# A retention layer and two gated layers on one core: two batches' attention and u ahead of their v, in a listed order

## The chip, the cores and the metric

The kernel runs on one core of a Trainium2 chip. The metric is the device time of one execution in microseconds, as the median of several runs. The core's engines (TensorE, VectorE, ScalarE, GpSimd, SyncE; PE, DVE, ACT, POOL, SP in the rows) run their own instruction lists in order and wait for each other by semaphores.

## The reference

Eight batches of 576 tokens, eight heads of 64; all in float32 (the weights come as float64).

```python
scores = scale * np.matmul(q, k.transpose(0, 1, 3, 2))
Dmat = np.where(rel >= 0, gamma[:, None, None] ** rel[None, :, :], 0.0)
x = transpose(np.matmul(scores * Dmat, v))        # [8, 576, 512]
h = gelu_tanh(x @ w_in)                           # 512 -> 1024
u, v = h[..., :512], h[..., 512:]
v_n = (v - mean(v)) / np.sqrt(var(v) + 1e-06) * g_ln
v_s = np.einsum('ts,bsd->btd', w_sg, v_n) + b_sg[None, :, None]
x = x + (u * v_s) @ w_out
gate = sigmoid(causal_conv(x, conv_w))            # 5 taps
out = gate * (x @ w_val) @ w_out2
```

## The kernel before, in words

Every product is made in float32r with the operands split into a high and a low part: high times high, high times low, low times high, so 12 matmuls for 512 input columns. The float64 weights are decoded to such pairs on the chip (`decode`, L122): two passes on ScalarE (absolute value, and the copy of the high part) and eight on VectorE.

**First part** (to about 440 us), for each batch:
- *Attention* in three groups of 192 tokens (group i is batch i // 3), in chunks of 64 tokens. Per group: `load_kq` and `load_v` (two buffers each), `k_decay` (12 or 8 small ScalarE operations), `q_decay`, `scores` (the products q k, tile sc, and the chunks' state sums, tile st), `masked` (sc by the decay mask, tile pt, one buffer), `states`, `state_decay` (all VectorE), `outputs` (tile xo, one PSUM buffer), `out_copy` (ScalarE, to the one staging buffer xg), `out_high` (ScalarE, the high part of x, and the store x1d, issued by SyncE), `out_low` (VectorE). `burst(i)` (L381) is outputs of group i, then scores of group i + 1.
- *u*: eight tiles (`u_tile`, 12 matmuls of 288 columns, and `u_gelu`). Tile n takes a quarter of a half of w_in's columns and one half of the tokens; quarters 0 and 1 of w_in (256 columns each) hold u, quarters 2 and 3 hold v.
- *v*: four tiles of 128 tokens, and one for the last 64 tokens of two batches (`v_tile`, 12 matmuls of 512 columns), each with gelu, statistics (VectorE and GpSimd), normalisation and split; vt has two buffers.
- *Mix*: eight tiles (`mix`, 14 matmuls of 288 columns, over w_sg split in ws and wr) and `gate` (VectorE), stored to g1d.

The two PSUM buffers of `ps_g` serve all tiles of u, v and mix.

**The order.** The head is written out by hand (L507 to L642): decode of quarter 0, attention of groups 0 to 2 between the decodes of quarters 1 to 3, the eight u tiles of batch 0, and v of batch 0 between the bursts of groups 3 and 4. From there a planner (`plan`, L641) gives every step a place in TensorE's time and sorts: the list `slow` (v and u of batch 1, then for each batch b mix b, v and u of b + 2), with the bursts at the places of `PLACES`, counted in steps from mix b. The planner also puts the split of w_sg into v of batch 1 and the decode of the second weights (`decode_second`, two of twelve pieces of w_out, w_val, w_out2 per batch) into u.

**Second part**: nine blocks of 512 tokens with the three remaining products, the convolution and the gate. TensorE never waits there until the end.

Of the kernel before, what the change touches and what calls it, by code (L numbers as in the profile page):

```python
# [44 lines left out]
def fused_kernel(  # L45
# [48 lines left out]
    with ExitStack() as p1:  # L94
# [23 lines left out]
        ws = one.tile([128, 2, 4, S], F32R, name="ws")  # L118
# [3 lines left out]
        def decode(dst_hi, dst_lo, src, a, s, t, like=lambda x: x):  # L122

            low, high = src[:, :, 0], src[:, :, 1]
            af, sf, tf = a.bitcast(F32), s.bitcast(F32), t.bitcast(F32)

            yield act.activation(af, high.bitcast(F32), AF.Abs)
            dve.tensor_scalar(af, af, _as_f32(896 << 20), _as_f32((1150 << 20) + 0xFF000), op0=ALU.max, op1=ALU.min)

            dve.tensor_scalar(a, a, 3, 0x40000000, op0=ALU.logical_shift_left, op1=ALU.bitwise_xor)  # L130
            dve.tensor_scalar(s, high, 31, 31, op0=ALU.logical_shift_right, op1=ALU.logical_shift_left)
            yield dve.scalar_tensor_tensor(a, a, 0x7FFFF000, s, op0=ALU.bitwise_and, op1=ALU.bitwise_or)

            dve.tensor_scalar(t, high, 0x1FF, None, op0=ALU.bitwise_and)
            yield dve.scalar_tensor_tensor(tf, t, 2.0**32, low, op0=ALU.mult, op1=ALU.add)
            dve.tensor_scalar(s, a, 23, 23, op0=ALU.logical_shift_right, op1=ALU.logical_shift_left)
            yield dve.scalar_tensor_tensor(dst_lo, like(tf), 2.0**-52, like(sf), op0=ALU.mult, op1=ALU.mult)
            yield act.copy(dst_hi, like(af))

        def run(steps, n=9):  # L140
            for _ in range(n):
                if next(steps, None) is None:
                    break
# [5 lines left out]
        def fetch_w_in(g):  # L149
            sync.dma_start(out=raw_in[:, g % 2].rearrange("p n t -> p (n t)"), in_=w_in[g])  # L150

        def decode_w_in(g):
            cols = slice(g * 256, (g + 1) * 256)
            return decode(
                wi[:, 0, :, cols],
                wi[:, 1, :, cols],
                raw_in[:, g % 2],
                *(tmp_in[:, i] for i in range(3)),
                like=lambda x: x.rearrange("p (k c) -> p k c", k=KT),
            )  # L160
# [4 lines left out]
        raws = {}  # L165
# [6 lines left out]
        def load_conv():  # L172
            n = KT * TAPS
            both = dec.tile([128, 2, n], F32, tag="cw", name="cw")
            run(decode(both[:, 0], both[:, 1], raws.pop("conv")[:, :n], *small_tmp(n)))
            dve.tensor_tensor(cw_sb.rearrange("p k t -> p (k t)"), both[:, 0], both[:, 1], op=ALU.add)
# [4 lines left out]
        def decode_second(j):  # L181
            raw = raws.pop(j)
            t = raw.rearrange("p n t -> p (n t)").rearrange("p (t n) -> p t n", t=2).bitcast(F32)
            yield from decode(t[:, 0].bitcast(F32R), t[:, 1].bitcast(F32R), raw, *small_tmp(DM))
            yield sync.dma_start(out=w2d[:, j // KT, :, j % KT], in_=t)
# [28 lines left out]
        def load_kq(i):  # L214
            if i < NGR:
                t = grp[i] = {}
# [35 lines left out]
        def scores(i):  # L252
# [4 lines left out]
            a, k, v = t["a"], t["k"], t["v"]  # L257
            st = t["st"] = ps_a.tile([128, 2, 512], F32, tag="st", name="st")
            sc = t["sc"] = ps_a.tile([128, 2, 512], F32, tag="sc", name="sc")
            for j in range(GC):  # L260
                at = slice(j * CK, (j + 1) * CK)
                for f in range(2):
                    for o, c in four:
# [5 lines left out]
                        )  # L269
            for j in range(chunks(i)):  # L270
# [86 lines left out]
        def out_high(i):  # L357
            b, g = divmod(i, NG)
            if g == 0:
                x = bt[b] = dict(  # L360
                    xh=mid.tile([128, KT, S], F32R, tag="xh", name="xh"),
                    xl=mid.tile([128, KT, S], F32R, tag="xl", name="xl"),
                )
                x["xr"] = (
                    bt[b - 1]["xr"]
                    if b % 2
                    else [mid.tile([128, KT, 128], F32R, tag=f"xr{j}", name="xr") for j in range(2)]
                )
# [3 lines left out]
            sync.dma_start(out=x1d[:, :, b * S + g * GT : b * S + (g + 1) * GT], in_=xc)  # L372
# [97 lines left out]
        mx = {}  # L470

        def mix(b, i):
# [3 lines left out]
            vh, vr = t["vh"], t["vr"]  # L476
# [3 lines left out]
            for s in range(4):  # L480
                a, l = vh[:, 0, s, cols], vh[:, 1, s, cols]
                wh, wl = ws[:, 0, s, t0 : t0 + n], ws[:, 1, s, t0 : t0 + n]
                for lhs, rhs in ((a, wh), (a, wl), (l, wh)):
                    pe.matmul(ps[:, :n], lhs, rhs, start=first, stop=False)  # L484
                    first = False
            for j in range(2):
                pe.matmul(ps[:, :n], vr[:, cols], wr[:, j, t0 : t0 + n], start=False, stop=j == 1)  # L487
# [17 lines left out]


        fetch_w_in(0)  # L507
        sync.dma_start(out=kf_sb, in_=kfac)
        load_kq(0)
        sync.dma_start(out=dm_sb, in_=dmask)  # L510
        load_v(0)
        sync.dma_start(out=qf_sb, in_=qfac)
# [472 lines left out]
```

## Time and profile before

| | us |
|---|---|
| median of 3 runs | 759.81 (759.77 to 760.47) |
| profiled execution | 759.48 |
| its span, first to last instruction | 757.6 |
| TensorE busy in the span | 723.0 |
| VectorE busy | 513.7 |
| ScalarE busy | 332.5 |

Mean granted clock of TensorE: 0.981 of 2.4 GHz. TensorE is busy in 95% of the span, and the rest is not spread evenly: in the page's 40 slices, those after 125 us show it busy throughout and at full clock, and those before show gaps and, from 15 to 45 us and around 80 and 91 us, the lower clock. Busy time counts a matmul at the lower clock at its full length.

### The profile page before, as it was taken

To read this page: it belongs to the slowest core of one execution; us is meant where nothing else is said; L and a number is where in the kernel's file an instruction comes from. 1 tells how busy PE (TensorE), PEld (TensorE's weight loads), DVE (VectorE), ACT (ScalarE), POOL (GpSimd) and SP (SyncE) were. 2 spreads that over 40 slices of the span, in tenths; PEclk is the share of its full clock that TensorE was granted. 3 is DMA by queue.
4 is the path that set the end of the run, shared out by engine and by line. 5 is a ranking of instruction groups with operands and counts; after the bars stand their busy time and mean duration, and the time that the engine had idled before them with its cause. 6 is when DMAs were issued, how large, how long until landed. Compare 5 with 4: busy or idle time off the path is not lost.

```text
span 757.6 us, 18035 instructions
## 1 busy us (share of the span) xinstructions
PE 723.0 (95%) x7804; PEld 631.8 (83%) x7804; DVE 513.7 (68%) x890; ACT 332.5 (44%) x638; POOL 51.4 (7%) x123
## 2 busy tenths in 40 slices
PE   6499789999999999999999999999999999999998
PEld 6487679989899799898998998888888888888886
DVE  5964658676576686775764369997876858667512
ACT  4545854454452734653336206444543425243321
POOL 0001120020210200301103000000000000000000
PEclk9689899999999999999999999999999999999999
DMA  9963745848518658476143683331404322010111
GB/s 357 380 197 128 241 152 181 298 163 285 178 62 278 213 181 301 134 250 240 56 138 134 249 291 141 136 143 56 166 32 136 93 75 104 7 56 1 55 56 55
DMA packets 54718, 121.21 MB, mean 160 GB/s; under 512 B 3952, under 2 KB 25584, under 8 KB 53744
## 3 DMA queue, kind: packets, MB, share of 16 engines
q1 hardware_dynamic: 49024, 104.87, 40.6%
q10 hardware_dynamic: 5184, 8.92, 3.1%
q0 software_dynamic: 432, 6.29, 2.2%
q8 instruction: 61, 1.00, 0.5%
q14 instruction: 17, 0.14, 0.1%
HBM read 85.46 MB, written 34.60 MB: 158 GB/s over the span
## 4 chain that ended last, share of the span: by engine, by line
PE 81%; DVE 5%; ACT 5%; DMA 4%; issue 2%; POOL 1%; SPq 0%; ACTq 0%; DVEq 0%; POOLq 0%
PE ps_back L89 13%; PE ps_out L89 13%; PE ps_val L89 13%; PE ps_m L484 13%; PE ps_u L89 12%; PE ps_v L395 8%; PE ps_m L487 2%; PE xo L335 2%; PE xo L327 2%; DMA qk_sb<-in_qk 2%; PE sc L265 2%; PE st L274 2%; DMA x1d<-xg 1%; ACT vt L429 1%; ACT vt L412 1%
## 5 line engine op out<-in xcount | busy, mean ns | idle before, releaser
L89 PE MATMUL ps_u<-xh,wi 128*128 128x288 f32 x512 | 108.9, 302 | 6.9 <-ACT vt L412 4.7
L484 PE MATMUL ps_m<-ws,vh 128*128 128x288 f32 x768 | 113.5, 296 | 0.1
L834 DVE SCALAR_TENSOR_TENSOR gate<-x,cw_sb,gate 128x516 f32<-128x516 f32 (+1 forms) x144 | 103.3, 748 | 6.2 <-ACT gate L832 5.1
L484 PEld LDWEIGHTS ps_m<-ws,vh 128*128 128x128 f32 x768 | 105.1, 188 | 1.2 <-DVE gt L494 0.6
L89 PE MATMUL ps_out<-gv,wv 128*128 128x512 f32 x432 | 102.3, 395 | 0.0
L89 PE MATMUL ps_val<-xs,wv 128*128 128x512 f32 x432 | 102.3, 395 | 0.0
L89 PE MATMUL ps_back<-gs,wo 128*128 128x512 f32 x432 | 102.0, 395 | 0.0
L89 PEld LDWEIGHTS ps_val<-xs,wv 128*128 128x128 f32 x432 | 81.3, 188 | 19.3
L89 PEld LDWEIGHTS ps_out<-gv,wv 128*128 128x128 f32 x432 | 81.3, 188 | 19.2
L89 PEld LDWEIGHTS ps_back<-gs,wo 128*128 128x128 f32 x432 | 81.1, 188 | 19.5
L89 PEld LDWEIGHTS ps_u<-xh,wi 128*128 128x128 f32 x512 | 85.1, 192 | 9.9 <-ACT vt L412 6.0
L395 PE MATMUL ps_v<-wi,xh 128*128 128x512 f32 x256 | 83.1, 407 | 3.0 <-ACT xh L69 1.5
L89 PE MATMUL ps_u<-xl,wi 128*128 128x288 f32 x256 | 76.7, 300 | 2.2 <-DVE xl L72 2.2
L395 PEld LDWEIGHTS ps_v<-wi,xh 128*128 128x128 f32 x256 | 48.5, 194 | 14.3 <-ACT xh L69 2.1
L494 DVE SCALAR_TENSOR_TENSOR gt<-ps_m,g_sb,b_sb 128x288 f32<-128x288 f32 x64 | 33.0, 516 | 40.3 <-PE ps_m L487 40.3
L849 DVE TENSOR_TENSOR gvf<-ps_val,gate 128x512 f32<-128x512 f32 (+7 forms) x64 | 26.6, 452 | 47.5 <-PE ps_val L89 47.5
L832 ACT ACTIVATE gate<-x,cw_sb 128x516 f32<-128x516 f32 (+1 forms) x36 | 25.9, 725 | 64.0 <-DVE x L815 64.0
L69 ACT CAST gv<-gvf 128x512 fp32r<-128x512 f32 x36 | 22.3, 620 | 68.6 <-DVE gvf L849 67.6
L420 DVE BATCH_NORM_STATS2 stat<-vt 128x6 f32<-128x512 f32 x36 | 25.0, 693 | 40.4 <-ACT vt L412 40.2
L395 PE MATMUL ps_v<-wi,xl 128*128 128x512 f32 x128 | 51.5, 402 | 0.3 <-DVE xl L72 0.3
L412 ACT ACTIVATE vt<-ps_v 128x512 f32<-128x512 f32 x36 | 21.5, 597 | 68.4 <-PE ps_v L395 61.3
L89 PEld LDWEIGHTS ps_u<-xl,wi 128*128 128x128 f32 x256 | 49.1, 192 | 2.7 <-DVE xl L72 2.5
(88 smaller groups left out, 1012.4 us busy)
## 6 DMA issues: line engine op xcount, KB each, us to landing
qk_sb<-in_qk SPq DMA_DIRECT2D x24, 960.0 KB, 7.9
vv_sb<-in_vv SPq DMA_DIRECT2D x24, 576.0 KB, 4.3
kk_sb<-in_kk SPq DMA_DIRECT2D x24, 384.0 KB, 5.1
x1d<-xg SPq DMA_DIRECT2D x24, 384.0 KB, 7.4
g1d<-u SPq DMA_DIRECT2D x16, 576.0 KB, 6.7
graw<-g1d SPq DMA_DIRECT2D x9, 1024.0 KB, 5.6
xraw<-x1d SPq DMA_DIRECT2D x9, 1024.0 KB, 5.1
out<-o ACTq DMA_DIRECT2D x32, 256.0 KB, 2.0
```

What stands on the lines that cost most here:

```text
L69: return act.copy(dst, src) if engine is act else engine.tensor_copy(dst, src)
L89: pe.matmul(ps[:, :n], lhs, rhs[:, k, x_cols], start=i == 0, stop=i == last)
L265: pe.matmul(sc[half[c], o, (2 * j + f) * CK : (2 * j + f + 1) * CK], a[half[o], 6 + 2 * x + f, at], a[half[o], 2 - 2 * x + f, at], start=T ...
L274: pe.matmul(st[half[c], o, (2 * j + f) * D : (2 * j + f + 1) * D], k[half[o], j, 2 * x + f], v[half[o], j, 2 * x + f], start=True, stop=Tr ...
L395: pe.matmul(ps, lhs, rhs, start=i == 0, stop=i == KT * 3 - 1)
L412: act.activation(vt, vs[b, s][0], AF.Gelu_apprx_tanh)
L420: dve.bn_stats(stat, vt)
L484: pe.matmul(ps[:, :n], lhs, rhs, start=first, stop=False)
L494: dve.scalar_tensor_tensor(gt, mx.pop((b, i))[:, :n], g_sb[:, m : m + 1], b_sb[:, t0 : t0 + n], op0=ALU.mult, op1=ALU.add)
L832: act.mul(gt, x2[:, m, a:z], cw_sb[:, m, 0:1])
L834: last = dve.scalar_tensor_tensor(gt, x2[:, m, a + j : z + j], cw_sb[:, m, j : j + 1], gt, op0=ALU.mult, op1=ALU.add)
L849: dve.tensor_tensor(gv[:, a:z], ps[:, a:z], t["gate"][:, m, a + o : z + o], op=ALU.mult)
```

## The change

- *Order of the head.* The hand-written order is replaced by one from a list scheduling, written out step by step (some 170 lines): attention of groups 0 to 5 and scores of group 6, and between them all u tiles of batch 0 and batch 1; then v of both batches, from the planner. The decode's ten steps (now a list of functions) are spread singly. w_in's quarter 0 comes in two pieces. `scores` is cut in two (`scores` and `adds`).
- *Batch 0's x* lies in a buffer `x1_sb` with the tag of ws. So w_sg's split begins when v of batch 0 has read it; it sits in the planned v of batch 1, and its high part is made by VectorE.
- *The store of x1d* is issued by ScalarE's queue, behind `out_high`.
- *Mix* issues its last two matmuls (wr) as a step of its own, `mix_rest`, at place + 1.62.
- *Bursts* have new places; the second weights are fetched and decoded one batch later.
- The warm-up is 50 matmuls of 64 columns instead of 30 of 128; conv_w has a buffer of its own.

```diff
+WARM = 50
 PLACES = [
-    ((-2, 4, 9), (-2, 4, 9)), ((-5, 1, 7), (-5, 1, 7)), ((1, 7, 10), (1, 7, 12)),
-    ((-2, 4, 9), (-2, 4, 9)), ((-6, 1, 6), (-6, 1, 6)), ((3, 7, 10), (3, 7, 10)),
+    ((0, 4, 8), (2, 6, 8)), ((-6, 0, 4), (-6, 0, 4)),
+    ((0, 5, 9), (0, 5, 9)), ((-5, 2, 7), (-5, 2, 7)),
+    ((2, 7, 10), (2, 7, 12)), ((0, 4, 7), (0, 4, 7)),
 ]
...
-        ws = one.tile([128, 2, 4, S], F32R, name="ws")
+        x1_sb = one.tile([128, 2, KT, S], F32R, tag="ws", name="x1_sb")
...
         def split_w_sg(k):
             r = raws.pop(("sg", k))
+            if k == 0:
+                mx["ws"] = one.tile([128, 2, 4, S], F32R, tag="ws", name="ws")
+            ws = mx["ws"]
             high, low = (ws[:, 0, k], ws[:, 1, k]) if k < 4 else (wr[:, 0], wr[:, 1])
-            hi(act, high, r)
+            hi(dve, high, r)
...
         def out_high(i):
...
+                if b == 0:
+                    x = bt[b] = dict(xh=x1_sb[:, 0], xl=x1_sb[:, 1])
...
-            sync.dma_start(out=x1d[:, :, b * S + g * GT : b * S + (g + 1) * GT], in_=xc)
+            act.dma_start(out=x1d[:, :, b * S + g * GT : b * S + (g + 1) * GT], in_=xc)
...
+        u_tile(0, 2)
+        k_decay(3, act, (0,))
         q_decay(3)
-        burst(2)
+        k_decay(3, act, (2,))
+        d[2][5]()
+        u_tile(0, 0)
+        u_gelu(0, 2)
...
+        outputs(5)
+        u_gelu(1, 0)
+        k_decay(6, act, (2,))
+        q_decay(6)
+        scores(6, False)
...
                 at(start, mix, *args)
+                at(start + 1.62, mix_rest, *args)
                 at(now + 0.1, gate, *args)
...
         def jobs(b):
-            return range(2 * b - 2, min(2 * b, 3 * KT)) if b else ()
+            return range(2 * b - 4, 2 * b - 2)
...
-        slow = [("v", 1, s) for s in range(5)] + [("u", 1, n) for n in range(2 * KT)]
-        bursts = {1: [("o", 5), ("s", 6)]}
+        slow = [("v", 0, s) for s in range(4)] + [("v", 1, s) for s in (4, 0, 1, 2, 3)]
+        bursts = {}
...
+        for k in range(5):
+            at(13.9 + 2.79 * k, split_w_sg, k)
             if k < 3:
-                at(4.1 + 2.79 * x, fetch_w_sg, k + 2)
+                at(13.91 + 2.79 * k, fetch_w_sg, k + 2)
```

What the order shows at three places (the columns are line, operation, output tile and operands, shape, count; x_sb is x1_sb).

TensorE's list where v starts. Before, the last u tile of batch 0 and then v(0,0):

```order
L89 MATMUL ps_u<-xh,wi 128x288 x2
L89 MATMUL ps_u<-xl,wi 128x288
L89 MATMUL ps_u<-xh,wi 128x288 x2
L89 MATMUL ps_u<-xl,wi 128x288
L89 MATMUL ps_u<-xh,wi 128x288
L395 MATMUL ps_v<-wi,xh 128x512 x2
L395 MATMUL ps_v<-wi,xl 128x512
L395 MATMUL ps_v<-wi,xh 128x512 x2
L395 MATMUL ps_v<-wi,xl 128x512
L395 MATMUL ps_v<-wi,xh 128x512 x2
```

Now, the last u tile of batch 1 (u(1,6)), then four v tiles of batch 0, the tile of both batches' last tokens, and v of batch 1:

```order
L91 MATMUL ps_u<-xl,wi 128x288
L91 MATMUL ps_u<-xh,wi 128x288 x2
L91 MATMUL ps_u<-xl,wi 128x288
L91 MATMUL ps_u<-xh,wi 128x288
L424 MATMUL ps_v<-wi,x_sb 128x512 x48
L424 MATMUL ps_v<-wi,xr 128x512 x12
L424 MATMUL ps_v<-wi,xh 128x512 x2
L424 MATMUL ps_v<-wi,xl 128x512
L424 MATMUL ps_v<-wi,xh 128x512 x2
```

The u tiles of batch 1 have moved ahead of all of v, and all nine v tiles of two batches stand in one row without a burst between them.

ScalarE's list from the first group's outputs on. Before:

```order
L244 ACTIVATE kk_sb<-kk_sb,kf_sb 128x64 x12
L344 COPY xg<-xo 128x2x2x192
L69 CAST xh<-xg 128x4x192
L138 CAST wi<-tmp_in 128x4x256
L244 ACTIVATE kk_sb<-kk_sb,kf_sb 128x64 x8
L127 ACTIVATE tmp_in<-raw_in 128x1024
L344 COPY xg<-xo 128x2x2x192
L69 CAST xh<-xg 128x4x192
```

Now:

```order
L129 ACTIVATE tmp_in<-raw_in 128x1024
L370 COPY xg<-xo 128x2x2x192
L71 CAST x_sb<-xg 128x4x192
L401 DMA x1d<-xg 512x1x192
L264 ACTIVATE kk_sb<-kk_sb,kf_sb 128x64 x8
L370 COPY xg<-xo 128x2x2x192
L71 CAST x_sb<-xg 128x4x192
L401 DMA x1d<-xg 512x1x192
```

The store of x1d stands in ScalarE's own list, and the first copy of group 1's outputs to xg comes one decay behind it; the pass of the decode stands ahead of the first copy.

VectorE's list in v, where w_sg is split (ws). Before, in the end of batch 0's v and the start of batch 1's:

```order
L72 TENSOR_TENSOR vh<-vt,vh 128x512
L72 TENSOR_TENSOR xl<-xg,xh 128x4x192
L72 TENSOR_TENSOR ws<-raw,ws 128x576
L250 TENSOR_TENSOR qp<-qk_sb,qf_sb 128x4x128
L420 BN_STATS stat<-vt 128x6
L421 BN_AGGR mv<-stat 128x2
L72 TENSOR_TENSOR ws<-raw,ws 128x576
L285 TENSOR_TENSOR pt<-sc,dm_sb 128x768
L309 COPY sums<-st 128x256
L307 TENSOR_TENSOR sums<-st,sums 128x256 x2
L72 TENSOR_TENSOR ws<-raw,ws 128x576
```

Now, from the low half of v(0,2) on:

```order
L74 TENSOR_TENSOR vh<-vt,vh 128x512
L71 CAST ws<-raw 128x576
L74 TENSOR_TENSOR ws<-raw,ws 128x576
L449 BN_STATS stat<-vt 128x6
L450 BN_AGGR mv<-stat 128x2
L74 TENSOR_TENSOR vh<-vt,vh 128x512
L71 CAST ws<-raw 128x576
L74 TENSOR_TENSOR ws<-raw,ws 128x576
L449 BN_STATS stat<-vt 128x6
L450 BN_AGGR mv<-stat 128x2
L74 TENSOR_TENSOR vr<-vt,vr 64x512 x2
L71 CAST ws<-raw 128x576
```

Each split is now two operations of VectorE, and they stand between the statistics and low halves of five successive v tiles, where before the attention of groups 4 and 5 stood between them.

## Rows read from the trace of the kernel before

**Rows 1.** The page, busy time, share and instructions of each engine.

```profile
PE 723.0 (95%) x7804; PEld 631.8 (83%) x7804; DVE 513.7 (68%) x890; ACT 332.5 (44%) x638; POOL 51.4 (7%) x123
```

**Rows 2.** Stretches: length, busy PE, PEld, DVE, ACT, POOL (instructions), PE clock, DMA share, GB/s.

```profile
0.00:9.96 9.96, 8.91 (x61) 8.79 (x61) 3.29 (x6) 5.34 (x14) 0.20 (x4) 1.00 0.81 311
9.96:34.39 24.43, 11.96 (x449) 11.07 (x449) 21.47 (x31) 12.36 (x29) 0.00 (x0) 0.75 1.00 402
34.39:60.00 25.61, 20.91 (x288) 19.36 (x288) 18.50 (x26) 12.25 (x27) 0.00 (x0) 0.83 0.61 203
60.00:124.34 64.34, 56.08 (x924) 47.31 (x925) 39.51 (x79) 38.77 (x85) 11.29 (x27) 0.95 0.50 163
124.34:440.00 315.66, 311.36 (x4701) 289.92 (x4700) 208.91 (x398) 141.90 (x307) 39.08 (x85) 1.00 0.60 202
```

**Rows 3.** Timeline of TensorE: start, length, instruction, count [idle before, releaser].

```profile
37.62 0.68 PE L89 MATMUL ps_u<-xh,wi 128*128 128x288 f32 x2
...
38.34 0.68 PE L89 MATMUL ps_u<-xh,wi 128*128 128x288 f32 x2
...
60.00 0.73 PE L395 MATMUL ps_v<-wi,xh 128*128 128x512 f32 x2 [1.43 <-ACT wi L138]
...
65.78 0.40 PE L335 MATMUL xo<-pt,vv_sb 64*64 64x64 f32 x12
...
118.32 0.46 PE L335 MATMUL xo<-pt,vv_sb 64*64 64x64 f32 x16
...
119.53 0.88 PE L265 MATMUL sc<-qk_sb 64*64 64x64 f32 x48
...
121.06 0.40 PE L89 MATMUL ps_u<-xh,wi 128*128 128x288 f32 x1
...
124.34 0.83 PE L484 MATMUL ps_m<-ws,vh 128*128 128x288 f32 x5
```

**Rows 4.** Who TensorE waits for, whole span: us in all, times, longest.

```profile
PE xo L335 <- DVE pt L285: 7.3, 2, 4.0
...
PE st L274 <- issue: 6.5, 3, 3.1
...
PE ps_u L89 <- ACT vt L412: 4.7, 4, 2.9
```

**Rows 5.** Timeline of VectorE, 5 to 60 us; then tile ws, 80 to 105 us.

```profile
6.77 0.69 DVE L128 TENSOR_SCALAR tmp_in<-tmp_in 128x1024 f32<-128x1024 f32 x1 [5.76 <-ACT tmp_in L127]
...
13.70 0.68 DVE L250 TENSOR_TENSOR qp<-qk_sb,qf_sb 128x512 f32<-128x512 f32 x1
...
14.30 0.95 DVE L285 TENSOR_TENSOR pt<-sc,dm_sb 128x768 f32<-128x768 f32 x1
...
19.05 0.96 DVE L250 TENSOR_TENSOR qp<-qk_sb,qf_sb 128x768 f32<-128x768 f32 x1 [2.54 <-DMA qk_sb<-in_qk]
...
26.18 1.33 DVE L307 TENSOR_TENSOR sums<-st,sums 128x256 f32<-128x256 f32 x3
...
27.43 0.95 DVE L72 TENSOR_TENSOR xl<-xg,xh 128x768 fp32r<-128x768 f32 x1
...
45.37 0.96 DVE L285 TENSOR_TENSOR pt<-sc,dm_sb 128x768 f32<-128x768 f32 x1 [3.88 <-PE sc L265]
...
48.91 0.42 DVE L309 COPY sums<-st 128x256 f32<-128x256 f32 x1 [2.59 <-PE st L274]
...
L72 DVE TENSOR_TENSOR ws<-raw,ws x4: 747/754/757, 85.2 to 97.5; 128x576 fp32r<-128x576 f32 x4
```

**Rows 6.** DMA: landing of xg's store; out at 560 to 575, 575 to 590; w_sg.

```profile
DMA to landing us min/median/max: 3.0/6.8/9.5
...
out<-o ACTq DMA_DIRECT2D x2, 256.0 KB, 5.7
...
out<-o ACTq DMA_DIRECT2D x2, 256.0 KB, 2.0
...
raw<-in_w_sg SPq DMA_DIRECT2D x1, 288.0 KB, 5.0
```

More of the change, by code (lines that the diff above doesn't have):

```diff
@@ L519, in fused_kernel @@
         warm = ps_g.tile([128, 512], F32, tag="g", name="warm")
-        for _ in range(30):
-            pe.matmul(warm[:, :128], zero, zero, start=True, stop=True)
-        d = [decode_w_in(g) for g in range(4)]
-        run(d[0], 1)
-        k_decay(0)
-        run(d[0])
-        fetch_w_in(2)
+        for _ in range(WARM):
+            pe.matmul(warm[:, :64], zero, zero[:, :64], start=True, stop=True)
+        d = [decode_w_in(0, 0, 1), decode_w_in(0, 1, 4)] + [decode_w_in(g) for g in range(1, 4)]
@@ new lines, in fused_kernel @@
+        d[0][4]()
+        d[1][9]()
+        d[0][5]()
+        d[0][9]()
+        d[0][6]()
+        d[0][7]()
+        d[1][5]()
+        scores(0, False)
+        k_decay(0, act, (0,))
+        d[1][6]()
+        k_decay(0, act, (1,))
+        masked(0)
+        k_decay(0, act, (2,))
+        d[0][8]()
+        d[1][7]()
+        adds(0)
+        d[1][8]()
+        scores(1, False)
+        k_decay(1, act, (2,))
+        states(0)
+        k_decay(1, act, (0,))
+        q_decay(1)
+        k_decay(1, act, (1,))
@@ L546, in fused_kernel @@
-        fetch_w_in(3)
-        k_decay(2)
+        outputs(1)
+        k_decay(2, act, (1,))
         q_decay(2)
-        burst(1)
+        scores(2, False)
+        load_v(3)
+        d[2][1]()
+        k_decay(2, act, (0,))
+        d[2][2]()
+        adds(2)
+        masked(2)
         load_kq(4)
-        run(d[2], 2)
-        state_decay(2)
-        masked(2)
+        out_copy(1)
         states(2)
-        out_copy(1)
         out_high(1)
-        out_low(1)
-        for n in (0, 2):
-            u_tile(0, n)
-            u_gelu(0, n)
@@ L561, in fused_kernel @@
-        run(d[2])
-        run(d[3], 1)
-        k_decay(3)
-        q_decay(3)
-        burst(2)
+        d[2][3]()
+        outputs(2)
+        d[2][4]()
+        k_decay(3, act, (1,))
+        scores(3, False)
+        load_v(4)
+        out_low(1)
+        fetch_w_in(2)
+        d[2][9]()
+        masked(3)
+        u_tile(0, 2)
+        k_decay(3, act, (0,))
+        q_decay(3)
+        k_decay(3, act, (2,))
+        d[2][5]()
+        u_tile(0, 0)
+        u_gelu(0, 2)
+        d[2][6]()
@@ L566, in fused_kernel @@
+        adds(3)
+        d[2][7]()
+        out_copy(2)
+        d[2][8]()
         load_kq(5)
-        out_copy(2)
-        masked(3)
+        scores(4, False)
+        k_decay(4, act, (1,))
         states(3)
+        u_tile(0, 6)
+        k_decay(4, act, (2,))
         state_decay(4)
         out_high(2)
+        q_decay(4)
+        outputs(3)
+        k_decay(4, act, (0,))
         out_low(2)
-        for n in (4, 6):
-            u_tile(0, n)
-            u_gelu(0, n)
-        run(d[3], 3)
@@ L577, in fused_kernel @@
-        for n in range(1, 8, 2):
-            u_tile(0, n)
-            u_gelu(0, n)
-        run(d[3])
-        q_decay(4)
+        u_gelu(0, 0)
+        adds(4)
+        load_v(5)
+        fetch_w_in(3)
+        u_gelu(0, 6)
+        masked(4)
+        u_tile(0, 7)
+        load_kq(6)
+        states(4)
+        d[3][0]()
+        u_tile(0, 4)
+        state_decay(5)
+        u_gelu(0, 7)
+        d[3][1]()
+        out_copy(3)
+        d[3][2]()
+        out_high(3)
+        u_tile(0, 5)
+        d[3][3]()
@@ new lines, in fused_kernel @@
+        u_gelu(0, 4)
+        d[3][4]()
+        k_decay(5, act, (0,))
+        u_tile(0, 1)
+        out_low(3)
+        d[3][9]()
+        outputs(4)
+        q_decay(5)
+        u_gelu(0, 5)
+        u_gelu(0, 1)
+        k_decay(5, act, (1,))
+        d[3][5]()
+        scores(5, False)
+        d[3][6]()
+        out_copy(4)
+        adds(5)
+        out_high(4)
+        masked(5)
+        u_tile(0, 3)
+        out_low(4)
+        states(5)
+        u_tile(1, 0)
+        u_gelu(0, 3)
+        d[3][7]()
@@ L682, in plan @@
                 if args[1] == 0:
[L683 removed]
+                    decode_at(i, now)
                 if args[1] == 2 * KT - 1:
```

285 lines of the change are left out of this document (155 added, 130 removed).

## The prediction, made before the changed kernel ran

> **What bounds the kernel now.** I read the page first, then the stretches, then who TensorE waits for, then the timelines of TensorE and VectorE. The page says that TensorE is busy 723.0 of 757.6 us [rows 1], so a change of order can at best win the other 34.6 us and what the low clock costs. The stretches say where that is [rows 2]: after 124.34 us, where the first mix starts, TensorE lacks 4.3 us up to 440 us, at clock 1.00. Ahead of it, it lacks 26.5 us of 124.34, and the clock is 0.75 and 0.83 in the stretches from 9.96 to 60.00 us. So everything worth having lies ahead of the first mix.
>
> There TensorE waits for VectorE and for what VectorE feeds [rows 4]: masked scores (7.3 us), the gelu of v (4.7 us, named as ScalarE's, which itself waits there for VectorE), and 6.5 us for which the profile shows no releaser. VectorE is busy 21.47 of 24.43 us in the second stretch [rows 2], when it decodes w_in between the groups of the attention. One decode of a quarter of w_in takes it from 6.77 to 13.70, 6.93 us [rows 5]. The v part can't start before the last quarter, and it starts at 60.00 [rows 3]; TensorE then has 64.3 us up to the first mix, for work that takes far less at the full clock. That is the gap the change goes for: batch 1's u needs only the first two quarters and can fill the time in which the other two are decoded.
>
> **The sum**, in the span of the profiled execution.
>
> *Term 1, the start of v(0,0): from 60.00 to 72.5, a loss of 12.5.* In the new order VectorE has, up to the last step of the last decode, the four decodes (27.7) and the attention's share of groups 0 to 6. By the times from one start to the next [rows 5], which are 0.08 under an instruction's own: masked scores 0.87 x 7 = 6.1; sums 1.25 for three chunks and 0.83 for two, five and two times, 7.9; decayed q 0.6 x 3 (two chunks) + 0.87 x 4 = 5.3; state decay, as large as one sum, 0.42 x 4 = 1.7; low halves 0.87 x 6 and 0.42 x 2 = 6.1. Together 54.8. It can start 0.9 earlier than before, at 5.85, since the first piece of w_in is 768 KB instead of 1024 KB and both its landing (0.6 us at the 402 GB/s of [rows 2]) and its first pass on ScalarE shrink. So with no wait at all the decode ends at 60.7.
>
> Waits of VectorE I took by walking the three new orders against each other by hand, with the durations of [rows 3, 5] (attention matmuls at the low clock's lengths until the u tiles run). Group 0's q and k are now the last of 3.2 MB instead of 2.4 MB and land 1.8 us later at 402 GB/s, at about 10.7, so the scores start there; the first quarter is decoded at 14.2, the first outputs start at 17.8, the second at 20.9. Then come waits of 0.2 to 1.5 us, 5.7 in all (before, VectorE had three of 2.5 to 3.9 in this place, 9.0 in all [rows 5]).
>
> The one new wait is the store of x. It goes from SP's queue to ScalarE's, and the copy of the next group's outputs waits on ScalarE until the store before has left the one staging buffer. By the walk the first store is issued at 22.2 and the second copy could start at 26.0. Queued behind that copy on ScalarE are group 1's high half, group 3's decay of k and the cast of the second quarter; TensorE's third outputs wait for the copy (one PSUM buffer), VectorE for the high half. What a store on ScalarE's queue takes beside loads, no row shows for this tile. Bounds: on SP's queue it landed in 3.0 to 9.5 us; the output's 256 KB on ScalarE's queue took 2.0 alone and 5.7 beside a 1 MB load [rows 6]. The loads of groups 2 to 4 are in flight here, so I take the second, by size: 5.7 x 384 / 256 = 8.5. The copy then starts at 30.7, 4.7 late. With 3.0 it would cost nothing, with 9.5 it would cost 5.7. The Trainium skill (DMA: Bandwidth & Descriptors, section "Issuing engines are not separate DMA queues") says that transfers started by different engines run on the same 16 DMA engines and interleave, and that several issuers save only the issuing time. This speaks against a gain from the new queue; by it alone the store would take the old 9.5 and the sum would be 1.0 higher. The 5.7 against 2.0 of the output's stores agrees that they share.
>
> So VectorE's waits are 5.7 + 4.7 = 10.4, the last decode ends at 71.1, and TensorE, which by the walk is 1.4 behind it with its last u tile, starts v at 72.5. TensorE alone would not need that long: 16 u tiles at 1.64 us (two run from 121.06 to 124.34 [rows 3]) and the attention up to the sums of group 6, some 18 us, after 10.7, make 55 at the full clock. The loads, 17.9 MB at 402 GB/s, are 45 us; they don't bind.
>
> *Term 2, from v(0,0) to the first mix: from 64.3 to 27.2, a gain of 37.1.* What is left there is nine v tiles, at 2.89 us (two from 60.00 to 65.78 [rows 3]) 26.0, and one group's outputs, 1.2 (118.32 to 119.53). Before, the u of batch 1, four bursts of the attention and waits lay in it too. VectorE's work in this stretch: nine statistics at 0.8, eight low halves at 0.65, two of 0.7, one decayed q and k, and five splits of w_sg. A split now has its cast on VectorE instead of ScalarE: between 0.39, by size from the decode's one-input pass of 0.69 over 1024 columns, and 0.75, what the subtraction of the same 576 columns takes [rows 5]; I take 0.65, as the subtraction has the same operands but one. That is 7 for the splits and 22.5 of 27.2 in all, so it is hidden, with little to spare (second rival).
>
> *Term 3, scores and sums of group 7*, which before lay ahead of the first mix, come behind it: 119.53 to 121.06 [rows 3], a loss of 1.5.
>
> *Term 4, everything behind the first mix: 0.* The bursts stand elsewhere in each batch, the decode of the second weights comes one batch later, and the 24 stores of x are issued by ScalarE. VectorE is busy 208.9 of 315.7 us there and ScalarE 141.9 [rows 2], so these hide; the last batch gets two decodes that it had not, and should its order be too tight, I put up to 4 on it, as much as TensorE lacks now. The best case is that the 4.3 us that TensorE lacks go.
>
> The shorter warm-up and the later last two matmuls of a mix cost nothing: TensorE waits for the first scores' data anyway, and the two matmuls follow the same twelve.
>
> Sum: 757.6 + 12.5 - 37.1 + 1.5 = 734.5 of span. The profiled execution took 759.48, 1.9 more than its span, and the median of the runs is 0.3 above it: 736.7 us.
>
> **The rivals.**
>
> *No wait for the store.* If it lands within 4 us, or the second copy is held by something else, 4.7 go: 732.0. For it: the store no longer stands behind 1.3 MB of loads in its own queue. Against it: the 5.7 us.
>
> *w_sg comes late.* Its split can start only when v(0,3) has read batch 0's x, and there are two raw buffers, so pieces 2 and 4 are fetched after splits 0 and 2. A piece took up to 5.0 us to land [rows 6] and a split takes 1.4. The first split starts 13.9 us into the stretch by its place, the third then ends at 21.7 and the fifth at 28 to 30; TensorE needs it at 28.8. If VectorE lags by 2 to 3 us more, all mixes move: 740.
>
> *The waits double.* A list that fits its own durations closely passes each late event on to all engines. If VectorE's 9.0 us of before come back beside the new ones, v starts at 81.5: 745.7. For it: the 6.5 us without a releaser, up to 3.1 at a time [rows 4], could fall into the u tiles, which now have no slack on TensorE. Against it: two thirds of the 9.0 were waits for scores and sums that the new order gives earlier.
>
> *The clock stays low* (slower than before). At 1.2 GHz a u matmul takes 0.24 us instead of 0.137 (three in 0.72 us from 37.62 on [rows 3]). Some 34 us of TensorE's work lie between the first u tile, at about 36, and v; at the low clock they are 60, with 2 us of waits v starts at 98, and the time is 757.6 + 38 - 37.1 + 1.5 + 2.2 = 762.2. It decides at 95.6: a v that starts later than that loses. For it: 0.75 and 0.83 in the same stretches before, when a u tile stood between short bursts [rows 2]. Against it: the clock came back to 2.4 GHz before when u tiles ran one after the other, and it is 0.95 in the mixed stretch after 60 us.
>
> That the change does nothing is no case: the new orders show the u tiles ahead of v.
>
> **How the numbers follow.** Forecast 0.50; store without wait 0.20; late w_sg 0.12; doubled waits 0.12; low clock 0.04; no difference from some other loss of 20 us 0.02. Two tenths of a per cent (1.5 us) is about what a measurement of this kernel can tell from none. The first four cases all win over 10 us: faster 0.94, same 0.02, slower 0.04. The range takes in the first rival with 4 us of term 4's gain, 728, and the third at the top, 746.
>
> **What would show it.** Right: the first ps_v at about 72 us, the first ps_m at about 100, u tiles of batch 1 at the full clock before v, VectorE nearly without idle from 6 to 71 apart from one wait of some 4 us near 26 us that begins with ScalarE's second copy. Term 1 is wrong if ps_v starts outside 67 to 82; term 2 if the stretch from ps_v to ps_m is longer than 30; term 4 if TensorE's idle from the first mix to the last 318 us differs from 4.3 by over 4. The forecast as a whole falls if v starts after 95.6, or if the time goes up behind the first mix.

## The result, and the profile after

The changed kernel takes 765.02 us (764.23 to 768.52) against 760.23 (759.77 to 761.41) for the kernel before on the same chip: a ratio of 1.0066, 95% interval 1.0045 to 1.0087. The forecast of 736.7 us, its range and its direction were wrong. The span of the profiled execution is 763.3 us; the sum had 734.5.

The stretches of the changed kernel, cut at the first scores, the first v and the first mix (columns as in [rows 2]):

```profile
0.00:22.58 22.58, 21.53 (x101) 21.41 (x101) 6.02 (x15) 9.48 (x29) 0.20 (x4) 1.00 0.77 291
22.58:92.53 69.95, 52.59 (x1378) 49.85 (x1377) 49.71 (x73) 35.51 (x88) 0.00 (x0) 0.88 0.73 254
92.53:120.68 28.15, 26.81 (x191) 21.32 (x189) 17.72 (x33) 14.25 (x23) 11.91 (x21) 1.00 0.20 65
120.68:763.30 642.62, 628.77 (x6186) 547.20 (x6180) 443.63 (x782) 271.87 (x496) 43.97 (x98) 1.00 0.43 147
```

and the last stretch of the kernel before, which answers to the fourth row:

```profile
124.34:757.60 633.26, 625.16 (x6086) 545.25 (x6084) 430.94 (x751) 263.79 (x484) 39.86 (x92) 1.00 0.43 146
```

The second row holds 52.6 us of TensorE's work in 70.0, and it starts only at 22.58. The third is as forecast: 28.15 us from v to the first mix (27.2 in the sum). So the first mix comes at 120.68 against 124.34 [rows 3], 3.7 earlier; and what follows it takes 9.4 longer. The timeline of TensorE shows the first loss:

```profile
1.05 21.59 PE L548 MATMUL warm<-zero 128*128 128x64 f32 x100 [1.05 <-DVE nh_sb L545]
22.58 1.56 PE L284 MATMUL sc<-qk_sb 64*64 64x64 f32 x48
...
92.53 0.86 PE L424 MATMUL ps_v<-wi,x_sb 128*128 128x512 f32 x3
...
123.14 0.40 PE L519 MATMUL ps_m<-wr,vr 128*128 128x288 f32 x1 [0.60 <-DVE wr L71]
123.94 0.40 PE L519 MATMUL ps_m<-wr,vr 128*128 128x288 f32 x1 [0.40 <-DVE wr L74]
```

The warm-up of 50 narrow matmuls (100 passes) lasts 21.6 us, 0.216 a pass; the first scores behind it wait for no data (no releaser), and take 1.56 us, where w50x128 below takes 0.93 for them. The timeline of ScalarE shows the second:

```profile
31.95 0.80 ACT L370 COPY xg<-xo 128x768 f32<-128x768 f32 x1 [4.78 <-PE xo L361]
...
32.79 0.59 ACTq L401 DMA_DIRECT2D x1d<-xg  x1
...
47.49 0.80 ACT L370 COPY xg<-xo 128x768 f32<-128x768 f32 x1 [11.95 <-DMA x1d<-xg]
...
73.62 0.80 ACT L370 COPY xg<-xo 128x768 f32<-128x768 f32 x1 [3.77 <-DMA x1d<-xg]
```

The store issued at 32.79 lands 14.6 us later by the issues of that stretch, and the second copy waits 11.95 us for it; the fifth copy waits 3.77 for the fourth store. Such a wait is not new: in the kernel before, where the first store took 9.5 us, the second copy shows

```profile
32.67 0.80 ACT L344 COPY xg<-xo 128x768 f32<-128x768 f32 x1 [2.44 <-DMA x1d<-xg]
```

TensorE's waits over the whole span of the changed kernel pass it on:

```profile
PE xo L353 <- ACT xg L370: 11.5, 2, 10.6
PE sc L284 <- issue: 4.0, 3, 2.0
PE ps_u L91 <- ACT u L497: 3.4, 3, 1.4
PE st L300 <- issue: 2.3, 1, 2.3
PE ps_v L424 <- ACT vt L441: 1.3, 1, 1.3
```

### The profile page after: what moved, and what is told of

Same layout as the page of the kernel before. It is cut to its first block, busy times and chain, and to the rows that moved or that the text cites. A ratio compares the mean times of both kernels' runs of the same rounds, so it can differ in the third digit from the quotient of the medians.

```text
span 763.3 us, 18106 instructions
## 1 busy us (share of the span) xinstructions
PE 729.7 (96%) x7844; PEld 639.8 (84%) x7844; DVE 517.1 (68%) x903; ACT 331.1 (43%) x635; POOL 56.1 (7%) x123
## 4 chain that ended last, share of the span: by engine, by line
PE 80%; ACT 6%; DVE 5%; DMA 4%; POOL 2%; issue 2%; ACTq 0%; DVEq 0%; POOLq 0%
PE ps_out L91 13%; PE ps_val L91 13%; PE ps_back L91 12%; PE ps_m L511 12%; PE ps_u L91 11%; PE ps_v L424 6%; PE warm L548 3%; PE sc L284 2%; PE xo L361 2%; PE xo L353 2%; DMA graw<-g1d 2%; PE st L300 2%; DMA x1d<-xg 2%; PE ps_m L519 2%; ACT vt L458 2%
## 5 line engine op out<-in xcount | busy, mean ns | idle before, releaser
L91 PE MATMUL ps_u<-xh,wi 128*128 128x288 f32 x448 | 92.7, 297 | 4.2 <-ACT u L497 3.4
L91 PEld LDWEIGHTS ps_u<-xh,wi 128*128 128x128 f32 x448 | 72.6, 188 | 6.0 <-ACT u L497 4.1
L424 PE MATMUL ps_v<-wi,xh 128*128 128x512 f32 x224 | 70.6, 396 | 1.3 <-ACT vt L441 1.3
L91 PE MATMUL ps_u<-xl,wi 128*128 128x288 f32 x224 | 66.1, 295 | 0.0
L370 ACT COPY xg<-xo 128x768 f32<-128x768 f32 x24 | 19.1, 797 | 88.8 <-PE xo L361 57.9
L424 PEld LDWEIGHTS ps_v<-wi,xh 128*128 128x128 f32 x224 | 41.5, 188 | 11.2 <-ACT vt L441 1.8
L264 ACT ACTIVATE kk_sb<-kk_sb,kf_sb 128x64 f32<-128x64 f32 x184 | 46.7, 336 | 0.0
```

Of the source, the lines that this page charges most:

```text
L91: pe.matmul(ps[:, :n], lhs, rhs[:, k, x_cols], start=i == 0, stop=i == last)
L264: act.mul(k[:, j, n], k[:, j, n], kf_sb[:, j, n : n + 1])
L424: pe.matmul(ps, lhs, rhs, start=i == 0, stop=i == KT * 3 - 1)
```

## The experiments

The kernel before was run beside every group of kernels, with medians of 760.2 to 760.8 us. The theory after the first look: the warm-up (W), the wait for the first store (S) and something behind the first mix make up the loss. A second theory (A, the place of the pieces of TensorE's instruction list) came out of the first kernels.

### w30x128: the old warm-up

```diff
-WARM = 50
+WARM = 30
-            pe.matmul(warm[:, :64], zero, zero[:, :64], start=True, stop=True)
+            pe.matmul(warm[:, :128], zero, zero, start=True, stop=True)
```

> The changed kernel with the old warm-up (30 matmuls of 128 columns). Theory W (the new warm-up ends at 22.6 us and holds the first scores, whose data are there by some 11 us): the warm-up ends at about 10, the first scores start at 10 to 11.5, v(0,0) comes 8 to 12 us earlier than 92.5, and the time falls by as much, to 753 to 757. Rival D (the first scores wait for the load of q and k, which is now the last of 3.2 MB): the scores start at 20 or later and the time stays at 764 to 766.

Measured: 764.44 us (761.06 to 771.41), ratio 1.0052 (1.0025 to 1.0078). The scores come at 12.62, where their data land, and v at 83.54, 9.0 us earlier than in the changed kernel; but the span from v on takes 680.3 us instead of 763.3 - 92.53 = 670.8. The time fits D, but not its mechanism: the loss sits elsewhere. TensorE's waits in this kernel:

```profile
PE st L300 <- issue: 10.0, 4, 4.0
...
PE sc L284 <- issue: 2.8, 3, 2.0
```

And its timeline, at two of the places behind v:

```profile
288.64 0.21 PE L284 MATMUL sc<-qk_sb 64*64 64x64 f32 x1 [2.04 <-issue]
...
384.74 0.47 PE L300 MATMUL st<-vv_sb,kk_sb 64*64 64x64 f32 x17 [1.49 <-issue]
```

TensorE stops in the middle of a burst's list and nothing in the profile releases it. The two kernels differ ahead of their bursts by 20 matmuls, that is 40 passes with a weight load each, 80 instructions. In the changed kernel the queue of the instructions moved 61 packets and 1.00 MB, which is 16 KB a packet and some 64 bytes for each of TensorE's 15,688 instructions (7844 passes, 7844 loads). Behind v, w30x128 has three such stalls of 0.9 us or more, 4.8 us together, and the changed kernel one of 1.4. That is 3.4 of the 9.5 us; TensorE's busy time behind the first mix is 3.3 higher too, and how this and the rest follow from the stalls was not traced.

### store_qf: the first six stores read a constant tile

```diff
-            act.dma_start(out=x1d[:, :, b * S + g * GT : b * S + (g + 1) * GT], in_=xc)
+            act.dma_start(out=x1d[:, :, b * S + g * GT : b * S + (g + 1) * GT], in_=xc if i > 5 else qf_sb)
```

> The changed kernel, but the store of x1d for groups 0 to 5 reads a constant tile of the same size (so the x of the first two batches that the second part reads is not the reference's); the store's bytes and queue stay, only the staging buffer is not held by it. Theory S (the 10.6 us for which TensorE waits on ScalarE's second copy are the store holding the staging buffer): that copy runs right behind the second outputs, at about 36 instead of 47.5 us, v(0,0) comes 7 to 11 us earlier, and the time is 754 to 758. Rival L (the loads of groups 2 to 4, issued late behind the warm-up, bind there anyway): v(0,0) moves by less than 3 us and the time is 762 to 766.

Measured: 756.59 us (756.02 to 757.52), ratio 0.9946 (0.9925 to 0.9966). The stores are still made, with the same bytes, but no copy waits for them (x of the first two batches is not what is stored), as ScalarE's copies show:

```profile
31.54 0.80 ACT L370 COPY xg<-xo 128x768 f32<-128x768 f32 x1 [4.35 <-PE xo L361]
35.83 0.80 ACT L370 COPY xg<-xo 128x768 f32<-128x768 f32 x1 [0.70 <-PE xo L361]
```

The second copy comes at 35.83 instead of 47.49, and v at 85.29 instead of 92.53. The waits for stores are 7 to 8 us of the loss: S is right that stores hold the copies. The edit takes the fifth copy's wait away with the second's, so the 7 to 8 us are not the first store's alone.

### w30_store_qf: both

The two edits together.

> Both of these edits (again the stores of groups 0 to 5 read a constant tile). Theories W and S together, adding up: v(0,0) at 70 to 75 us, as the prediction had it, and the time 743 to 748, which is the predicted 736.7 and the 7.9 us that the stretch behind the first mix takes more than forecast. Rival: the two overlap (the store is slow only because the late loads all come at once), so the pair gains no more than 3 us beyond the better of the two, about 752.

Measured: 764.01 us (761.33 to 771.49), ratio 1.0046 (1.0013 to 1.0079). Neither theory foresaw this. With 30 warm-up matmuls the time stays at 764, with the store's wait or without it; v starts at 83.33, as with the wait, so the head loses elsewhere what the store gives back: the stalls of 0.9 us or more without a releaser ahead of v are five, 11.2 us, instead of three, 8.2. (The profiled execution took 771.49, the longest of ten.)

### w50x128: 50 matmuls at the old width

```diff
-            pe.matmul(warm[:, :64], zero, zero[:, :64], start=True, stop=True)
+            pe.matmul(warm[:, :128], zero, zero, start=True, stop=True)
```

> The changed kernel with 50 warm-up matmuls of 128 columns instead of 64: the same number, twice the columns. If the narrow matmuls take 0.216 us a pass because the clock never rises under them, these 100 passes take 0.216 us for the first 4 to 5 us and 0.107 behind, and end at 12 to 14 us, so the time falls to 754 to 758. If the pass is bound by its weights at any clock, or the granted clock is full as its row says, they take as long or longer, the warm-up ends at 22 or later, and the time is 765 or more.

Measured: 755.46 us (752.4 to 757.82), ratio 0.9925 (0.99 to 0.995), faster than both kernels. The same number of instructions as in the changed kernel, twice the columns, and the warm-up is shorter. Tile warm in this kernel (length in ns least, median, most, of passes that overlap; first and last start):

```profile
L548 PE MATMUL warm<-zero x100: 274/275/580, 1.1 to 13.6; 128*128 128x128 f32 x100
```

The same tile in the changed kernel:

```profile
L548 PE MATMUL warm<-zero x100: 421/421/472, 1.1 to 22.2; 128*128 128x64 f32 x100
```

The scores start at 13.85 and take 0.93 us instead of 1.56. The store's wait is still there (6.50 us before the second copy at 33.30), v starts at 83.00 and the rest takes 670.7 us, as in the changed kernel. W is right, and with this length of the list nothing is lost behind v.

### w30_p20: 30 matmuls and 20 narrow ones

```diff
-        for _ in range(WARM):
-            pe.matmul(warm[:, :64], zero, zero[:, :64], start=True, stop=True)
+        for x in range(WARM + 20):
+            c = 128 if x < WARM else 16
+            pe.matmul(warm[:, :c], zero, zero[:, :c], start=True, stop=True)
```

with WARM = 30.

> The changed kernel with the old warm-up of 30 matmuls over 128 columns, and 20 more matmuls over 16 columns behind them, so that TensorE's list of instructions is as long before the first scores as with 50 matmuls, while the warm-up ends some 2 us earlier. Theory A (the 9.5 us that the kernel with 30 matmuls lost behind v, and its stalls without a releaser, come from where the pieces of TensorE's instruction list, 16 KB each, begin and end among the attention bursts): the stalls go back to the few of the kernel with 50 matmuls over 128 columns, v starts at 81 to 84 us, and the time is 752 to 757 us. Rival T (they come from the earlier start itself, by the loads and stores that then meet): it stays at 761 to 766 us.

Measured: 757.5 us (755.51 to 760.37), ratio 0.9962 (0.9935 to 0.999): half a microsecond above A's range and well below T's. From v (84.43) on it takes 671.3 us, the number of the kernels with 50, not 680.3. The 20 narrow matmuls bring back what the 30 alone had lost behind v. That speaks for the length of the list, but T could still say that the later start did it, since the first scores came only at 16.29: the 40 narrow passes took 5.9 us, and the scores 1.56 us, at a granted clock of 0.50.

### w40x128 and before_w40, before_w50: both orders with other lengths

In each only the number of warm-up matmuls, of 128 columns, is changed.

> The changed kernel with 40 warm-up matmuls over 128 columns: the warm-up ends near 11.8 us, before the first scores' data (12.6 us), and TensorE's list is 40 instructions longer than with 30 and 40 shorter than with 50. Theory A (where the pieces of the list begin sets the stalls, so that only the length counts): stalls at other places than with 30 or 50, 753 to 761 us. Rival (what counts is that the scores start as early as the data allow): 762 to 766 us, as with 30.

> The kernel before with 40 warm-up matmuls over 128 columns, for the comparison of the two orders at the same warm-up: with 30 the changed order took 3.7 us more than the kernel before (764.44 against 760.7), with 50 it took 11.2 us less (755.46 against 766.63). If a longer warm-up only costs what it lasts past the first scores' data: 760.5 to 763 us. Theory A: anything from 756 to 767 us, by where the stalls fall.

> The kernel before with 50 warm-up matmuls over 128 columns in place of 30: its first scores start some 4 us later, and its TensorE list is 80 instructions longer ahead of the bursts. If a longer warm-up only costs what it lasts, or the data come late anyway: 760 to 765 us. Theory A says that its stalls without a releaser (6.5 us before st) move too: if they shrink by more than the 4 us that the warm-up costs, 755 to 760 us, and if they grow, over 765 us.

| matmuls over 128 columns | kernel before | changed order |
|---|---|---|
| 30 | 760.2 to 760.8 | 764.44 (761.06 to 771.41) |
| 40 | 759.76 (758.72 to 764.0) | 757.42 (753.44 to 761.0) |
| 50 | 766.63 (765.53 to 767.17) | 755.46 (752.4 to 757.82) |

With 40 the scores start at 12.72, as early as with 30 (12.62), and from v (85.70) on it takes 673.2 us: the time is out of T's range and in A's, which was wide, and single executions run from 753 to 761. The kernel before loses 5.9 us with 50, though v starts at 60.72, only 0.7 later than before; 2.6 of the loss lie between v and the first mix, where it waits 7.0 us for a v tile's gelu, and 3.3 behind the mix. Neither expectation had this: the first ended at 765, and A wanted the stalls before st to grow for it, but they shrank (6.5 to 4.2 us). Their places count, not their sum: two of them, 1.4 us each, now end at 197.55 and 387.80, behind the mix, where the kernel before has none. The wait for the gelu is 6.75 us in before_w40 too; its profiled execution, 764.0 us, is the longest of its ten, so the median of 759.76 can't be read from that trace. The worth of the new order is a loss of 4 us or a gain of 11, by a few matmuls that compute nothing; with each order at its best length here it is 4.3 (755.46 against 759.76).

What the stalls have to do with the list can be read from the traces and the packets of the instruction queue. All 14 kernels together show 47 stalls of TensorE without a releaser that last 0.9 us or more. When all of TensorE's recorded instructions (passes, weight loads and the few of its sequencer) are numbered from the first, 40 of the 47 stop at a number that leaves 194 to 196 when it is divided by 256, so they lie whole multiples of 256 apart; and 256 instructions of 64 bytes are one packet of 16 KB. So these stalls come where the list passes from one packet to the next. Each of the 40 ends 1.2 to 1.6 us after a packet has come in: in w30x128 the stall of 4.00 us ends at 30.06 and the packet came in from 27.65 to 28.58; that of 3.19 us ends at 61.20, the packet from 58.83 to 59.71. 80 instructions more put other instructions of the bursts at these places. The other seven all stop at one instruction, the 496th (st of group 1, at 20 to 28 us); these the list does not explain. The Trainium skill (Runtime: NRT & Kernel Launch, section "Instruction fetch mechanics") says that an engine's list comes in blocks of 16 KiB, which its sequencer fetches ahead by DMA, and that this is mostly hidden. The size agrees with the packets; hidden it is not in bursts of 64x64 matmuls: 48 of them, with their loads 96 instructions, take 0.93 us, so a block lasts TensorE some 2.5 us (an estimate).

### w50_qf: w50x128 without the store's wait

The edits of w50x128 and store_qf together.

> The changed kernel with 50 warm-up matmuls over 128 columns, and for the first two batches the store of x reads a constant tile in place of the copied x, so that the next copy has no store to wait for (x of these two batches is then not what is stored). If the two losses add: ScalarE's second copy comes at 27 to 28.5 us in place of 33.30, v starts at 76 to 79 us in place of 83.00, and the time is 748 to 751 us. Rival (in the kernel with 50 over 128 the wait for the store is replaced by the next one, or stalls fall elsewhere): 754 us or more.

Measured: 747.17 us (746.31 to 748.92), ratio 0.9829 (0.981 to 0.9848), better than expected. ScalarE's first two copies:

```profile
23.65 0.80 ACT L370 COPY xg<-xo 128x768 f32<-128x768 f32 x1 [1.56 <-PE xo L361]
27.65 0.80 ACT L370 COPY xg<-xo 128x768 f32<-128x768 f32 x1 [0.41 <-PE xo L361]
```

And TensorE's v:

```profile
73.66 11.36 PE L424 MATMUL ps_v<-wi,x_sb 128*128 128x512 f32 x48
```

The two losses add: 765.02 - 747.17 = 17.9 us, where the single edits gave 9.6 and 8.4.

### w50_sp: the stores in SyncE's queue

```diff
-            act.dma_start(out=x1d[:, :, b * S + g * GT : b * S + (g + 1) * GT], in_=xc)
+            sync.dma_start(out=x1d[:, :, b * S + g * GT : b * S + (g + 1) * GT], in_=xc)
```

on w50x128.

> The changed kernel with 50 warm-up matmuls over 128 columns, and all stores of x issued by SyncE in its own queue in place of ScalarE's. If the store is slow because its queue shares the DMA engines with the loads of the other queue: in SyncE's queue it lands in 4 to 9.5 us, the second copy comes at 29 to 33 us, and the time is 751 to 756 us. Rival (the loads behind it in SyncE's list wait for the copy that it waits for, and their data come late): v starts at 84 us or later and the time is 757 to 762 us.

Measured: 759.08 us (757.09 to 764.63), ratio 0.9982 (0.9958 to 1.0007): the rival. The store is issued at 26.94, 1.5 us behind the copy, and lands 8.9 us later; on ScalarE's queue in w50x128 the first store was issued at 24.06 and landed 9.1 us later. In this pair the queue makes no difference to the store. That agrees with the Trainium skill's rule in the prediction (DMA: Bandwidth & Descriptors, section "Issuing engines are not separate DMA queues"). Over all the traces it is less clear: the first store took 7.5 to 9.5 us in the four kernels with SyncE's queue and 9.1 to 14.6 in the ten with ScalarE's. When it is issued does not explain that alone: issued at 25.02 and 25.89, in w50_alt_cast and w50_alt below, it took 13.2 and 9.3 us. What made it 14.6 in the changed kernel stays open. The time and v (84.69) are the rival's, and SyncE waits 17.9 us for the copies that its stores read, with loads behind them; but TensorE waits only some 1 us for loads ahead of v, and the scores start 1.3 later (15.17) of the 1.7 that v does, so the rival's mechanism is not shown. (The profiled execution took 764.63, the longest of ten; 3.9 us of it are one wait for gt behind the mix.)

### w50_alt and w50_alt_cast: versions that keep the result

```diff
-            t["xc"] = two.tile([128, KT, GT], F32, tag="xg", name="xg", bufs=1)
+            if i == 1:
+                t["xc"] = mid.tile([128, KT, S], F32, tag="xh", name="xg")[:, :, :GT]
+            else:
+                t["xc"] = two.tile([128, KT, GT], F32, tag="xg", name="xg", bufs=1)
```

on w50x128; the second has also

```diff
-            hi(dve, high, r)
+            hi(act, high, r)
```

> The changed kernel with 50 warm-up matmuls over 128 columns, and the copied x of group 1 alone goes to another buffer (batch 1's xh, not yet in use), so that ScalarE's second copy has no store to wait for, and all of x is stored. If the wait for the first store alone made the second loss: the second copy at 27 to 28.5 us, v at 73 to 77 us, 746 to 750 us. Rival (the third copy then waits for the first store, or group 3's xh for the second): 752 us or more.

> The same with the cast of w_sg's split back on ScalarE, as in the kernel before. If the cast on VectorE makes VectorE late for wr, gt, gs and xs (some 3 us of TensorE's waits behind the first mix): 1 to 2.5 us less than w50_alt. Rival (these waits are of the order of the work, not of the cast, or ScalarE is late for u in turn): within 0.8 us of w50_alt, or slower.

Measured: w50_alt 752.46 us (749.71 to 755.08), ratio 0.9894 (0.9867 to 0.9921); w50_alt_cast 747.78 us (746.68 to 752.51), ratio 0.9846 (0.9818 to 0.9874), the fastest of the versions that compute the reference. In w50_alt the second copy no longer waits (28.71), but v starts at 79.25, not at 73 to 77: the fifth copy still waits 4.32 us for the store before it, as it did in w50x128 (5.98), and TensorE stands 2.66 us until 34.99 without a releaser. The time lies in the rival's range, but not by its mechanism: neither the third copy nor group 3's xh waits for a store. The first store's wait alone was worth some 3 us of w50x128's time (the ranges overlap) and 3.8 of its start of v; the 8.3 and 9.3 of w50_qf are those of all six stores. The cast on ScalarE gave 4.7 us in the medians (the ranges overlap). In the spans it is 1.1 ahead of v and 3.0 behind it: 28.16 to 27.11 from v to the first mix, and 642.1 to 640.2 from there on, a little over the 2.5 that its theory allowed. Three rows of w50_alt's timeline of TensorE have nothing of their size in w50_alt_cast:

```profile
103.09 0.72 PE L427 MATMUL ps_v<-wi,xh 128*128 128x512 f32 x2 [1.33 <-ACT vt L444]
...
109.86 0.40 PE L522 MATMUL ps_m<-wr,vr 128*128 128x288 f32 x1 [0.59 <-DVE wr L71]
110.66 0.40 PE L522 MATMUL ps_m<-wr,vr 128*128 128x288 f32 x1 [0.40 <-DVE wr L74]
```

The stretch of w50_alt_cast behind the first mix is

```profile
105.22:745.40 640.18, 628.14 (x6187) 547.14 (x6180) 443.02 (x781) 271.20 (x496) 44.78 (x97) 1.00 0.43 148
```

and of its 12 us of TensorE's idle time these rows of the timeline are 5.3:

```profile
200.36 0.40 PE L91 MATMUL ps_u<-xh,wi 128*128 128x288 f32 x1 [1.39 <-ACT u L500]
...
300.76 0.40 PE L91 MATMUL ps_u<-xh,wi 128*128 128x288 f32 x1 [1.00 <-ACT u L500]
...
399.84 0.40 PE L91 MATMUL ps_u<-xh,wi 128*128 128x288 f32 x1 [1.00 <-ACT u L500]
...
448.97 1.19 PE L91 MATMUL ps_back<-gs,wo 128*128 128x512 f32 x4 [0.63 <-ACT gs L71]
451.07 1.19 PE L91 MATMUL ps_val<-xs,wv 128*128 128x512 f32 x4 [0.91 <-ACT xs L71]
452.66 10.50 PE L91 MATMUL ps_back<-gs,wo 128*128 128x512 f32 x44 [0.40 <-DVE gs L74]
```

## Why the prediction was wrong

The span came out 28.8 us above the sum: 20.0 in term 1, 0.9 in term 2, 7.9 in terms 3 and 4. Term 1 failed by its own sign, v outside 67 to 82 us. It was walked on VectorE, whose row up to the end of the last decode, with its longest waits, is

```profile
6.33:91.00 84.67, 67.31 (x1442) 64.46 (x1442) 55.21 (x86) 42.40 (x114) 0.00 (x0) 0.90 0.74 264
...
24.20 0.96 DVE L311 TENSOR_TENSOR pt<-sc,dm_sb 128x768 f32<-128x768 f32 x1 [10.14 <-PE sc L284]
...
49.18 0.96 DVE L74 TENSOR_TENSOR x_sb<-xg,x_sb 128x768 fp32r<-128x768 f32 x1 [8.63 <-ACT x_sb L71]
...
75.31 0.96 DVE L74 TENSOR_TENSOR xl<-xg,xh 128x768 fp32r<-128x768 f32 x1 [1.82 <-ACT xh L71]
```

Its work is 55.2 us against 54.8, and v follows 1.5 us behind it against 1.4. Its waits are 29.5 us against 10.4: 10.1 for the late scores, 8.6 and 1.8 behind the copies that wait for stores, and 8.9 of small ones.

- **"The shorter warm-up and the later last two matmuls of a mix cost nothing: TensorE waits for the first scores' data anyway"** is the step that failed most. Shorter was read off the columns (50 x 64 against 30 x 128), where [rows 2] gave a length for passes over 128 columns only. The warm-up lasts 21.6 us and the scores start at 22.58 instead of 10.7: 11.9 of the 20.0. Of these 1.9 are not the warm-up's: the data land at 12.6, as w30x128 shows. Wider matmuls (w50x128) gave back 9.6 us of the time.
- **Term 1, the store.** The mechanism was right (one staging buffer, the second copy waits, TensorE's outputs and VectorE's high half behind it), the size was not. The sum had 8.5 us from issue to landing and 4.7 of loss for the second copy alone; the store took 14.6 us, VectorE waited 8.6 for that copy and 1.8 for the fifth, which the sum left out, and without any store's wait v came 7.2 us earlier. It was not "the one new wait" either: the kernel before has it, with 2.44 us, and its 9.5 is this very store, issued at 23.06. So 9.5 was the nearest row, but no bound. By the Trainium skill's rule weighed there the store would take 9.5; w50_sp's 8.9 on SyncE's queue beside w50x128's 9.1 on ScalarE's agrees with it, the 9.1 to 14.6 of the other traces do not follow from it.
- **Term 1, the walk.** VectorE's work was right; the small waits were 8.9 us instead of 5.7, with the scores' and stores' waits taken out. In w50_qf, take the store's 4.7 out of 72.5 and add the later scores (14.46 instead of 10.7): 71.6, and v starts there at 73.66. That is closer than the walk was: the scores, 3.8 later, cost VectorE only 1.9 us. In store_qf the same working gives 79.7, and v starts at 85.29. The low clock stayed off most of the u tiles: in the changed kernel 48 of their matmuls take 6.65 us from 61.27 on, 0.14 each, and the slowest stretch, 12 from 73.17 on, takes 3.07.
- **Term 2** was right: 28.15 instead of 27.2. Its second rival (w_sg late) took place with a price of 2 to 3 us instead of the forecast's nothing: the waits of 1.33 for v's gelu and of 0.99 for wr go away with the cast on ScalarE. A cast on VectorE takes 0.45 us, inside the bounds, and VectorE is busy 17.7 us in this stretch, less than the 22.5 forecast; what was wrong is "hidden".
- **Terms 3 and 4.** The sum had 633.3 + 1.5 behind the first mix; it was 642.6. TensorE's idle rose from 8.1 to 13.9 us and its busy time by 3.6, of which 1.5 are group 7's. The rise of 5.8 is above the 4 that the sum allowed. The waits for u's gelu (3.4 us in three, before 1.3 in two) and at the start of the second part (some 2 us, before none) are the larger part of it; 2.1 us are stalls without a releaser. Each of the three waits for u stands at one place, where ScalarE's list has the last v tile's scaling and split ahead of two of u's gelus, and that scaling waits for GpSimd's rs:

```profile
215.79 0.82 ACT L458 ACTIVATE vt<-vt,rs 128x512 f32<-128x512 f32 x1 [1.54 <-POOL rs L453]
```

The kernel before has one such place, at 216.02 on TensorE, with 1.0 us. Another order there was not tried. The cast back on ScalarE takes 1.9 away; the other 6 us, 2.1 of busy time among them, are not shown by an experiment. The sign given for term 4 just missed the loss: up to the last 318 us the idle time is 8.1 us instead of 4.3.

- **The rivals.** The slower side was given to a low clock before v at 95.6. v did start close to it, at 92.53, but for two other reasons, and the clock of that stretch was 0.88. "The waits double" named the stalls without a releaser as what could fall into the u tiles; they fell into the bursts, most of them at places that the list's length sets, up to 4.0 us at a time.

So the thought of the forecast, that u of two batches fills the gap, holds in part: w50_alt_cast, the same order with another warm-up, a second place for group 1 and the cast on ScalarE, takes 747.8 us, 12.4 less than the kernel before. It remains 11 us above the forecast: 5.6 in the start of v (78.11) and 5.4 behind the first mix (640.2 instead of 634.8).

## What to carry to other kernels

Price every edit at the edge of a listed order by a row of the same shape; a warm-up over fewer columns has no row here, and it was longer. Where one staging buffer is written again after a transfer has read it, the transfer's length is in the chain, and the same transfer took 9 to 15 us here; a second place for one group gave some 3 us, another queue lost some 4. When one such wait is taken away, look for the next one: the fifth copy's was there all along. When a kernel has bursts of small matmuls, compare two orders at several lengths of the instruction list, or the difference of 4 to 11 us between them may be that of the list.

## What the runs showed of the hardware

- Passes of a float32 128x128 weight take 0.216 us over 64 columns for 21.6 us on end; over 128 columns they begin like that and later take about half (100 in 12.9 us). The profile's granted clock says 1.00 in the first stretch of both, where the lengths say otherwise; after the narrow passes the first scores took 1.56 us, after the wide ones 0.93.
- Passes of such a weight over 16 columns, in w30_p20, begin with 0.11 us and end with 0.21, as the granted clock falls from 1.00 to 0.50 at 13.4 us: a narrow pass is as long as a wide one at the same clock.
- The first store of 384 KB beside the loads took 9.1 to 14.6 us from ScalarE's queue (14.6 in the changed kernel, 9.1 in w50x128), and 7.5 to 9.5 from SyncE's.
- TensorE stops for 1 to 4 us in bursts of small matmuls, mostly where its list passes from one packet of 16 KB to the next (40 of 47 stalls in 14 traces), until 1.2 to 1.6 us after a packet has come in; 80 instructions more or fewer ahead of them move these stops, and the time by up to 9.
